# Last output tiles whole or in two column groups, warm-up products in banks of their own, and half of the last V copies ahead of q's transposition

## The chip, the cores and the metric

The kernel runs on one core of a Trainium2 chip. The time is that of the device, in microseconds, median of several executions; smaller is better. A core has five engines that run side by side and wait for each other through semaphores: TensorE (PE, matrix products; its loads of weights are shown as PEld), VectorE (DVE), ScalarE (ACT), GpSimd (POOL) and SyncE (SP, which here only issues DMAs). Products land in PSUM, which has 8 banks of 512 float32 values for each of 128 partitions; everything else lies in SBUF, and inputs and output in HBM.

## What is computed

Two blocks, one after the other. The first is an attention over 8 blocks of 96 positions, whose keys and values are mixed over blocks by a matrix P that five rounds of normalising rows and columns make (Sinkhorn). The second is a gated MLP whose gate is mixed over the positions:

```python
P = sort_net                                     # (4, 8, 8, 8)
for _ in range(5):
    P = exp(P - max(P, -1)); P /= sum(P, -1); P /= sum(P, -2)
k_s = einsum('bhij,bhjcd->bhicd', P, k_blocks)   # q, k, v: (4, 8, 768, 64)
v_s = einsum('bhij,bhjcd->bhicd', P, v_blocks)
x = softmax(q_blocks @ k_s.T / 8) @ v_s          # to (4, 768, 512)
u, v = split(relu(x @ w_in))                     # w_in (512, 1024)
v = (v - mean(v)) / sqrt(var(v) + 1e-6)
out = (u * (w_spatial @ v + b_spatial)) @ w_out  # (4, 768, 512), float32
```

## The kernel before

The work is cut into units, small functions named `u_XX`. The string ORDER (lines 16 to 48) lists them with their arguments, and the loop at the end of the kernel function calls them in that order; each engine gets its instructions in the order in which the units emit them, so ORDER is the schedule of every engine and queue at once. No planner changes it. A framework puts in semaphore waits where two instructions share a tile or a bank of PSUM. The first argument of most units is the first of the two PSUM banks they write (`ps_tile`, line 102), a letter says who copies the result out (A ScalarE, D VectorE, P GpSimd), then come the batch (0 to 3), and the head pair or chunk.

The four batches overlap: while batch 3 is in its attention, batch 2 is in its MLP. The units that matter here:

- `DM:bank:n:w` (L286) is n warm-up products of zeros ("dummies") of w columns. Nothing reads their result; they go to the first of the two banks.
- `SK` (L242) is one round of the normalisation on a tile of 32 x 64, on ScalarE (exp) and VectorE; the last one also transposes P. `PR`, `P0`, `PC`, `PD` spread P into the mixing matrices `pd`.
- `QT:bank:eng:b:hp:2` (L323) transposes q of one head pair by 12 products, over two banks. `KT` and `VT` (L338) mix and transpose k and v in one go. `LH:q:0:4:8` loads the second half of the first batch's q.
- `VM:bank:eng:b:hp` (L389) mixes v of a head pair, two products into two banks, and ScalarE or VectorE copies them to the tile `vm`. Each batch has four.
- `VC:b:ih` (L404) is four DMAs on SyncE's queue, which bring half of `vm` into the layout `vb` that the attention's second product reads; two VC make a batch. They need all four VM of the batch.
- `QX:eng:b` copies q to `qx` (L180, two instructions) and then issues a transposing DMA on SyncE's queue (L182) to `qX`. `XX:b:ih` is the transposing DMA of the attention's result (L189).
- `SC` (L422, exponential at L435) is the attention's first product, `AT` (L447) its second, which reads `vb`; `VP`, `UP` (L490, L535) are the products with w_in, `SP` (L547) and `SH` (L567) the mixing over positions with w_spatial, followed by the addition of the bias into `z` and the gate `gt` on VectorE or GpSimd. SP mixes a quarter of the channels over all positions, SH over half of the positions.
- The output of a batch is 6 chunks of 128 positions x 512 columns, each the sum of four products (mc 0 to 3) over `gt`. `OP` (L627) does two chunks at once. Only for the last batch `OF` (L588) does the first two products of a chunk ahead, while `gt` of mc 2 and 3 is not ready, and `OL` (L600) the other two, then a copy by ScalarE or VectorE and a store from SyncE's queue (L608). `OL:X` is the form for the very last chunk: ScalarE copies its left 256 columns and stores them from its own queue (L612, L614), VectorE the right 256, stored from SyncE's (L613, L615). `OH` (L617) is `OF` and `OL` of one chunk together; ORDER doesn't call it before.

On SyncE's queue near 85 to 105 us ORDER gives: XX:2:0, XX:2:1, QX:D:3, VC:3:1, VC:3:0. On PE in that place: SP:6:D:1:1, VM of head pair 2, SP:4:P:1:0, VM of pair 0, VM of pair 3, SP:0:P:1:2, two KT, VP, VM of pair 1, and two more VP. Of batch 3, the first AT reads half 1 of `vb`, the second half 0.

The last lines of ORDER hold the end: SP and SH of batch 3, then the chunks.

Of the kernel before, what the change touches and what calls it, by code (L numbers as in the profile page):

```python
# [8 lines left out]
FP32 = mybir.dt.float32  # L9
# [4 lines left out]


ORDER = """
IN LH:q:0:0:4 L:k:0:0:128 ID SK:0 MK SK:0 SK:0 QT:0:A:0:1:2 L:v:0:0:128 IV:1 SX DM:0:12:64
DM:1:12:64 DM:0:12:64 SK:0 SK:1 DM:1:12:64 QT:2:A:0:0:2 IV:0 LH:q:0:4:8 DM:0:12:64 PR:1 P0:0:2 L:wv
P0:4:6 P0:6:8 P0:2:4 L:wu L:v:1:0:128 PC:A L:k:1:0:128 L:ws DM:7:9:64 KT:2:D:0:0:2 KT:4:A:0:2:2
DM:7:2:64 KT:0:D:0:1:2 DM:7:1:64 VT:6:A:1:2 VT:2:D:0:2 SC:4:0:0:1 VT:0:D:2:2 PD:2:0:4 VX:7:D:1:1  # L20
QT:2:A:0:2:2 VX:4:A:0:1 VX:5:D:1:0 SC:0:0:1:1 VX:7:D:2:1 PD:1:0:4 PD:1:4:8 KT:2:D:0:3:2 PD:2:4:8
VX:4:D:0:0 PD:3:0:4 QT:6:A:0:3:2 VT:0:D:3:2 AT:2:P:0:0:1 L:q:1:0:128 SC:4:0:2:1 VX:7:D:2:0 SC:2:0:3:1
AT:0:D:0:1:1 SC:6:0:3:0 VX:4:D:3:1 VX:5:A:3:0 AT:2:D:0:2:1 SC:0:0:0:0 AT:6:D:0:3:1 XT:4:D:0:1:0
AT:2:P:0:3:0 SC:0:0:2:0 XT:7:D:0:1:1 L:v:2:0:128 AT:2:D:0:0:0 SC:4:0:1:0 AT:0:P:0:2:0 UP:6:A:0:0:1
AT:2:D:0:1:0 VP:0:A:0:5 VM:4:A:1:2 VM:6:D:1:1 XT:2:A:0:0:1 VM:0:D:1:0 XT:3:A:0:0:0 VP:4:A:0:3:4
VM:2:A:1:3 VP:0:A:0:2 VP:6:A:0:0:1 VC:1:0 LN:0:3:6 UP:2:A:0:1:1 L:k:2:0:128 WS:0:D:5 KT:6:A:1:1:2
KT:4:A:1:2:2 UP:2:A:0:0:0 LA:D:0:3 KT:6:D:1:0:2 PD:3:4:8 KT:4:A:1:3:2 QT:0:A:1:1:2 WS:2:D:4
QT:6:D:1:0:2 QT:4:A:1:2:2 QT:2:D:1:3:2 WS:0:D:3 LN:0:0:3 L:q:2:0:128 WS:1:D:0 SC:4:1:2:0 LA:P:0:5
LA:P:0:4 LA:P:0:1 SC:6:1:0:0 L:wo UP:2:D:0:1:0 VC:1:1 BB AT:0:P:1:2:0 AT:6:D:1:0:0 SC:4:1:1:0 SC:0:1:1:1
LA:P:0:2 VM:2:D:2:1 LA:P:0:0 VM:4:A:2:0 VM:6:D:2:2 SC:0:1:3:0 WS:2:D:2 SC:4:1:3:1 WS:3:D:1 VM:0:A:2:3  # L30
AT:6:D:1:1:0 AT:4:P:1:1:1 VC:2:0 SC:2:1:2:1 AT:0:D:1:3:1 AT:6:D:1:3:0 XX:1:0 SP:4:D:0:0 SC:0:1:0:1
AT:2:P:1:2:1 VC:2:1 QX:D:2 SP:6:D:0:2 AT:2:P:1:0:1 SP:4:D:0:1 SP:2:D:0:3 VP:6:A:1:0:1 KT:4:A:2:2:2
UP:0:A:1:1:0 KT:6:D:2:1:2 XX:1:1 KT:4:A:2:3:2 WT:x:1:1 L:v:3:0:128 KT:2:A:2:0:2 OP:0:D:0:0 SC:6:2:1:0
L:k:3:0:128 SC:2:2:2:0 VP:4:D:1:2:3 SC:2:2:2:1 SC:0:2:0:0 UP:6:A:1:1:1 AT:2:D:2:2:0 AT:4:P:2:1:0
LN:1:0:4 VP:0:A:1:4:5 UP:4:A:1:0:1 LA:D:1:2 SC:0:2:0:1 LA:P:1:3 SC:2:2:3:0 L:q:3:0:128 OP:6:A:0:2
LN:1:4:6 AT:0:D:2:0:0 AT:4:D:2:2:1 OP:2:D:0:1 LA:P:1:4 LA:D:1:5 LA:P:1:0 SC:0:2:1:1 SC:4:2:3:1
LA:D:1:1 UP:6:A:1:0:0 AT:0:D:2:0:1 AT:2:P:2:3:0 SP:4:D:1:3 AT:2:P:2:1:1 XX:2:0 AT:0:D:2:3:1
SP:6:D:1:1 VM:2:A:3:2 SP:4:P:1:0 VM:6:A:3:0 XX:2:1 VM:2:A:3:3 SP:0:P:1:2 QX:D:3 KT:2:A:3:3:2
KT:4:A:3:1:2 VP:6:A:2:0:1 VM:4:A:3:1 VP:2:A:2:4:5 VP:6:A:2:2:3 KT:2:A:3:0:2 KT:4:A:3:2:2 UP:0:A:2:0:1
LN:2:0:4 VC:3:1 UP:2:D:2:0:0 SC:4:3:3:0 LA:P:2:3 VC:3:0 SC:0:3:0:1 LA:D:2:2 UP:6:D:2:1:1 SC:4:3:3:1  # L40
SC:2:3:1:1 LA:D:2:1 UP:0:A:2:1:0 LA:P:2:0 AT:4:D:3:0:1 AT:6:D:3:3:0 LN:2:4:6 LA:P:2:4 OP:2:D:1:1
SC:4:3:1:0 SC:6:3:2:1 LA:D:2:5 OP:0:A:1:2 AT:6:D:3:2:1 AT:2:P:3:3:1 SP:4:D:2:0 AT:2:P:3:1:1
AT:6:P:3:1:0 SP:0:D:2:2 XX:3:1 SC:2:3:2:0 SC:4:3:0:0 OP:6:A:1:0 AT:0:D:3:0:0 AT:4:D:3:2:0 SP:2:P:2:1
SP:0:D:2:3 UP:2:A:3:1:1 VP:0:A:3:4:5 XX:3:0 UP:2:A:3:0:1 VP:4:A:3:2:3 LN:3:4:6 VP:2:A:3:0:1
OP:4:A:2:2 LA:P:3:4 LN:3:0:4 LA:P:3:3 LA:D:3:2 LA:D:3:0 LA:P:3:5 LA:P:3:1 UP:2:A:3:0:0 UP:0:A:3:1:0
OP:4:A:2:0 OP:0:A:2:1 SH:4:D:3:3:0 SP:2:D:3:0 SP:0:D:3:1 SP:2:D:3:2 SH:0:D:3:3:1 OF:1:3:1 OF:2:3:0
OF:3:3:2 OL:A:3:2 OL:D:3:0 OF:0:3:4 OL:D:3:4 OL:A:3:1 OF:2:3:3 OL:D:3:3 OF:0:3:5 OL:X:3:5
"""


# [9 lines left out]
def kernel(  # L60
# [12 lines left out]
    nc = tc.nc  # L73

    B, H, S, D = q.shape
# [5 lines left out]
    DM = H * D  # L81
# [3 lines left out]
    FC = DH // 128  # L85
# [9 lines left out]
    moe = ctx.enter_context(tc.tile_pool(name="moe", bufs=2))  # L95
# [3 lines left out]
    ps = psum.tile([128, 8, 512], FP32, name="ps")  # L99
    ps_bf = ps.rearrange("p x c -> p (x c)").bitcast(BF16).rearrange("p (x c) -> p x c", x=8)  # L100

    def ps_tile(n, dt=FP32):
        return (ps if dt == FP32 else ps_bf)[:, int(n):min(int(n) + 2, 8)]

    def copy(eng, out, in_):
        if eng == "A":
            nc.scalar.copy(out=out, in_=in_)  # L107
        else:
            nc.vector.tensor_copy(out=out, in_=in_)
# [26 lines left out]
    w_out_sb = const.tile([128, FC, DM], BF16, name="w_out_sb")  # L136
# [7 lines left out]
    st = {}  # L144
# [436 lines left out]
    def oh_mm(b, c, parts):  # L581
        for mc in parts:
            nc.tensor.matmul(  # L583
                st["oh", c][:, 0, :], lhsT=st["gt", b, mc][:, c * 128:(c + 1) * 128], rhs=w_out_sb[:, mc, :],
                start=(mc == EARLY[0]), stop=(mc == LATE[-1]),
            )
# [5 lines left out]
    def oh_tile():  # L592
        n = st["ohn"] = st.get("ohn", -1) + 1
        if n in (2, 3):
            return moe.tile([128, DM], FP32, name="oh_sb", tag="oh", bufs=2)
        if n % 2 == 0:
            st["oo"] = moe.tile([128, 2, DM], FP32, name="o_sb", tag="o", bufs=2)
        return st["oo"][:, n % 2]

    def u_OL(eng, b, c):  # L600
        b, c = int(b), int(c)
        oh_mm(b, c, LATE)
        t = st["oh", c][:, 0]
        o_sb = oh_tile()
        dst = out[b, c * 128:(c + 1) * 128, :]
        if eng in ("A", "D"):
            copy(eng, o_sb, t)
            nc.sync.dma_start(out=dst, in_=o_sb)  # L608
        else:
            h = DM // 2  # L610
            o2 = moe.tile([128, S], FP32, name="o2", tag="z", bufs=2)[:, 0:h]
            nc.scalar.copy(out=o_sb[:, 0:h], in_=t[:, 0:h])  # L612
            nc.vector.tensor_copy(out=o2, in_=t[:, h:DM])  # L613
            nc.scalar.dma_start(out=dst[:, 0:h], in_=o_sb[:, 0:h])  # L614
            nc.sync.dma_start(out=dst[:, h:DM], in_=o2)  # L615

    def u_OH(ps, eng, b, c):  # L617
        u_OF(ps, b, c)
        u_OL(eng, b, c)
# [55 lines left out]
```

## Time and profile before

| | |
|---|---|
| median of 3 runs | 157.74 us (157.69 to 157.99) |
| the profiled execution | 157.63 us |
| its span, first to last instruction | 155.9 us |
| PE busy | 140.2 us, 90% of the span |
| VectorE / ScalarE / GpSimd busy | 109.2 / 87.6 / 56.8 us |
| DMA | 25.50 MB, mean 164 GB/s; HBM read 24.78 MB, written 6.29 MB |
| granted PE clock over the span | 0.993 |

The difference of 1.7 us between the profiled execution and its span lies before the first and after the last instruction. "Busy" of PE counts a product as long as it is in the array; since products overlap, a busy PE is not one at its peak. Lines such as L447 are lines of the kernel; "SPq" or "ACTq" is the sequencer of an engine, which issues DMAs; `ps<-vb,ex` says what is written and read. In the timeline the columns are start and duration in us, engine, line, operation, tiles and the number of instructions; in brackets stands the idle time of the engine ahead, and what ended it.

### The profile page before, as it was taken

How to read it: one execution, taken by the hardware profiler on the slowest of the kernel's cores; microseconds unless marked ns; L12 is line 12 of the kernel's file. 1: busy time of each engine (PE TensorE's matmuls, PEld its weight loads, DVE VectorE, ACT ScalarE, POOL GpSimd, SP SyncE). 2: the span in 40 equal slices, each digit the busy share in tenths (PEclk: the TensorE clock that was granted, in tenths of full speed). 3: DMA queues.
4: the chain of work that ended last, by engine and by line, in shares of the span. 5: the costliest groups of instructions: out<-in, count | busy, mean ns of one | idle time of the engine just before them, and what ended most of it. 6: DMA issues, size and time to landing. Idle time of an engine off the chain costs nothing.

```text
span 155.9 us, 3816 instructions
## 1 busy us (share of the span) xinstructions
PE 140.2 (90%) x1553; PEld 87.6 (56%) x1564; DVE 109.2 (70%) x225; ACT 87.6 (56%) x132; POOL 56.8 (36%) x81
## 2 busy tenths in 40 slices
PE   0289999999989999999999999996999999999970
PEld 0188788646867665645556654663566554556520
DVE  3877889668789899648587958765568647328960
ACT  3224789888989430948864367983754247640030
POOL 7961944933146242022742271041051402610000
PEclk9999999999999999999999999999999999999997
DMA  2999999999999999979999934980438900342074
GB/s 14 194 203 207 204 205 204 210 207 206 247 275 206 205 229 229 201 131 143 204 196 267 264 55 81 173 158 3 155 114 132 209 0 0 135 165 109 0 263 145
DMA packets 36834, 25.50 MB, mean 164 GB/s; under 512 B 16592, under 2 KB 33744, under 8 KB 36816
## 3 DMA queue, kind: packets, MB, share of 16 engines
q0 software_dynamic: 14864, 12.19, 50.4%
q1 hardware_dynamic: 21808, 12.93, 34.3%
q8 instruction: 12, 0.20, 0.5%
q10 hardware_dynamic: 144, 0.13, 0.3%
q14 instruction: 6, 0.05, 0.1%
HBM read 24.78 MB, written 6.29 MB: 199 GB/s over the span
## 4 chain that ended last, share of the span: by engine, by line
PE 49%; DMA 25%; DVE 10%; POOL 4%; issue 4%; SPq 3%; ACT 1%; DVEq 0%; POOLq 0%; ACTq 0%
PE ps L547 13%; DMA v_in<-in_v_dram 12%; PE ps L627 9%; PE ps L490 8%; DMA q_in<-in_q_dram 8%; PE ps L535 6%; DVE z L553 4%; DVE gt L559 3%; PE ps L583 3%; PE ps L447 3%; DMA xT<-x_sb 3%; SPq L404 3%; DMA vb<-vm 2%; PE ps L422 2%; PE ps L389 1%
## 5 line engine op out<-in xcount | busy, mean ns | idle before, releaser
L547 PE MATMUL ps<-wspT,v_sb 128*128 128x384 bf16 x180 | 31.1, 326 | 0.0
L435 ACT ACTIVATE ex<-ps 96x768 bf16<-96x768 f32 x32 | 24.6, 806 | 9.2 <-PE ps L422 8.9
L459 POOL TENSOR_TENSOR x_sb<-xr,rec 96x512 bf16<-96x512 f32 x13 | 14.1, 1091 | 26.4 <-DVE rec L458 26.4
L535 PE MATMUL ps<-xT,w_in_sb 128*128 128x384 bf16 x128 | 23.2, 327 | 0.0
L547 PEld LDWEIGHTS <-v_sb 128*128 128x128 bf16 x180 | 17.0, 98 | 10.7
L490 PE MATMUL ps<-w_in_sb,xT 128*128 128x512 bf16 x91 | 22.1, 379 | 0.7 <-DMA xT<-x_sb 0.3
L504 DVE BATCH_NORM_STATS2 stats<-v_sb 128x6 f32<-128x512 bf16 x24 | 16.3, 677 | 8.4 <-ACT v_sb L113 8.3
L521 POOL TENSOR_SCALAR v_sb<-v_sb,nm,rstd 128x512 bf16<-128x512 bf16 x15 | 11.9, 792 | 20.1 <-ACT rstd L512 16.6
L553 DVE TENSOR_TENSOR z<-ps,b_bc 128x768 f32<-128x768 f32 x15 | 14.3, 956 | 6.2 <-PE ps L547 5.7
L113 ACT ACTIVATE v_sb<-ps 128x1024 bf16<-128x1024 f32 (+1 forms) x12 | 11.5, 954 | 9.9 <-PE ps L490 9.9
L627 PE MATMUL ps<-w_out_sb,gt 128*128 128x512 bf16 x67 | 16.6, 380 | 0.3
L535 PEld LDWEIGHTS <-w_in_sb 128*128 128x128 bf16 x128 | 11.8, 98 | 8.1
L490 PEld LDWEIGHTS <-xT 128*128 128x128 bf16 x96 | 8.9, 98 | 10.4 <-DMA xT<-x_sb 0.8
L113 ACT ACTIVATE u_sb<-ps 128x768 bf16<-128x768 f32 x13 | 10.5, 810 | 6.6 <-PE ps L535 6.1
L107 ACT COPY o_sb<-ps 128x1024 f32<-128x1024 f32 (+1 forms) x7 | 6.7, 952 | 12.3 <-DVE gt L576 8.8
L459 DVE TENSOR_TENSOR x_sb<-ps,rec 96x512 bf16<-96x512 f32 x19 | 13.0, 687 | 0.7
L447 PE MATMUL ps<-vb,ex 96*128 96x65 bf16 x256 | 11.7, 193 | 1.3 <-DMA vb<-vm 1.1
L447 PEld LDWEIGHTS <-ex 96*128 96x128 bf16 x256 | 10.2, 97 | 3.9 <-issue 1.2
L559 DVE TENSOR_TENSOR gt<-z,u_sb 128x768 bf16<-128x768 f32 x12 | 11.5, 958 | 0.4
L455 ACT COPY xr<-ps 96x520 f32<-96x520 f32 x13 | 7.6, 586 | 6.7 <-POOL x_sb L459 3.7
L323 PE MATMUL ps<-ident,q_in 128*64 128x128 bf16 x96 | 4.5, 244 | 6.9 <-DMA q_in<-in_q_dram 6.9
L627 PEld LDWEIGHTS <-gt 128*128 128x128 bf16 x72 | 6.6, 98 | 7.2
(91 smaller groups left out, 201.7 us busy)
## 6 DMA issues: line engine op xcount, KB each, us to landing
out_dram<-o_sb SPq DMA_DIRECT2D x9, 512.0 KB, 3.3
k_in<-in_k_dram POOLq DMA_DIRECT2D x4, 768.0 KB, 15.8
v_in<-in_v_dram POOLq DMA_DIRECT2D x4, 768.0 KB, 14.3
vb<-vm SPq DMA_DIRECT2D x24, 99.0 KB, 5.3
q_in<-in_q_dram POOLq DMA_DIRECT2D x3, 768.0 KB, 16.1
wsp_nat<-in_moe_w_spatial_dram POOLq DMA_DIRECT2D x1, 1152.0 KB, 25.7
w_in_sb<-in_moe_w_in_dram POOLq DMA_DIRECT2D x2, 512.0 KB, 13.9
q_in<-in_q_dram POOLq DMA_DIRECT2D x2, 384.0 KB, 8.5
```

Source lines behind the costliest of these rows:

```text
L113: nc.scalar.activation(out=out, in_=in_, func=AF.Relu)
L435: nc.scalar.activation(out=dst, in_=src, func=AF.Exp, scale=scale)
L447: nc.tensor.matmul(t[:, hh, ii * VW:ii * VW + D + 1], lhsT=e[:, c:c + 128], rhs=vb[b % 2][:, ih * NI + ii, 2 * hp + hh, 0:D + 1], start=Tr ...
L459: (nc.gpsimd if eng == "P" else nc.vector).tensor_mul(out=x_sb[:, hp].rearrange("p i (h d) -> p h i d", h=2), in0=tv[:, :, :, 0:D], in1=_r ...
L490: nc.tensor.matmul(t[:, x, :], lhsT=x_tile(b, n // 3)[:, kc, n % 3 * 128:(n % 3 + 1) * 128], rhs=w_in_sb[:, kc, DH:DFF], start=(kc == 0), ...
L504: nc.vector.bn_stats(out=stats, in_=v_sb[:, x, :])
L521: nc.gpsimd.tensor_scalar(out=v_sb, in0=v_sb, scalar1=nm[:, 0:1], scalar2=rs[:, n:n + 1], op0=ALU.add, op1=ALU.mult)
L535: nc.tensor.matmul(t[:, x, 0:HW], lhsT=w_in_sb[:, kc, mc * 128:(mc + 1) * 128], rhs=x_tile(b, ih)[:, kc], start=(kc == 0), stop=(kc == KC ...
L547: nc.tensor.matmul(t[:, x, 0:HW], lhsT=st["v_sb", b, n][:, mc * 128:(mc + 1) * 128], rhs=wspT[:, n, x * HW:(x + 1) * HW], start=(n == 0), ...
L553: nc.vector.tensor_add(out=z.rearrange("p (x c) -> p x c", x=2), in0=t[:, :, 0:HW], in1=b_bc.rearrange("p (x c) -> p x c", x=2),)
L559: eng.tensor_mul(out=gt, in0=z, in1=st["u", b, mc // 2][:, mc % 2])
L627: nc.tensor.matmul(t[:, x, :], lhsT=st["gt", b, mc][:, c * 128:(c + 1) * 128], rhs=w_out_sb[:, mc, :], start=(mc == 0), stop=(mc == FC - 1),)
```

## The change

Three parts, all by ORDER, the third with a new unit.

1. The dummies. There were 72: five groups of 12 in banks 0 and 1, which QT:0 and PR use too, and 9, 2 and 1 in bank 7 around the first KT. There are 60 now, in five groups in banks 4 and 5. The second QT comes ahead of all of them, and SK rounds stand otherwise in between.
2. VC:3:1 is issued ahead of QX:D:3. For that the VM of head pair 1 of batch 3 comes ahead of SP:0:P:1:2, in banks 6 and 7, where it was in banks 4 and 5 behind the first VP of batch 2.
3. The last chunks. Chunks 2, 0 and 1 are begun in OF and ended in OL as before, but in that order without others in between; chunks 4 and 3 are done whole (OH) in banks of their own, 4 and 5; chunk 5, the last, is done by the new unit OX in two groups of four products of 256 columns, the left in bank 6, the right in bank 7, each with its own copy and store. `OL` loses its form X.

```diff
 ORDER (pieces that differ)
-... IV:1 SX DM:0:12:64 DM:1:12:64 DM:0:12:64 SK:0 SK:1 DM:1:12:64 QT:2:A:0:0:2 IV:0
-    LH:q:0:4:8 DM:0:12:64 PR:1 P0:0:2 ...
+... IV:1 SX SK:0 QT:2:A:0:0:2 DM:4:12:64 DM:5:12:64 DM:4:12:64 DM:5:12:64 DM:4:12:64 SK:1 IV:0
+    LH:q:0:4:8 PR:1 P0:0:2 ...
-... L:ws DM:7:9:64 KT:2:D:0:0:2 KT:4:A:0:2:2 DM:7:2:64 KT:0:D:0:1:2 DM:7:1:64 VT:6:A:1:2 ...
+... L:ws KT:2:D:0:0:2 KT:4:A:0:2:2 KT:0:D:0:1:2 VT:6:A:1:2 ...
-... VM:6:A:3:0 XX:2:1 VM:2:A:3:3 SP:0:P:1:2 QX:D:3 KT:2:A:3:3:2 KT:4:A:3:1:2
-    VP:6:A:2:0:1 VM:4:A:3:1 VP:2:A:2:4:5 ... UP:0:A:2:0:1 LN:2:0:4 VC:3:1 UP:2:D:2:0:0 ...
+... VM:6:A:3:0 XX:2:1 VM:2:A:3:3 VM:6:A:3:1 SP:0:P:1:2 VC:3:1 QX:D:3 KT:2:A:3:3:2 KT:4:A:3:1:2
+    VP:6:A:2:0:1 VP:2:A:2:4:5 ... UP:0:A:2:0:1 LN:2:0:4 UP:2:D:2:0:0 ...
-... OF:3:3:2 OL:A:3:2 OL:D:3:0 OF:0:3:4 OL:D:3:4 OL:A:3:1 OF:2:3:3 OL:D:3:3 OF:0:3:5 OL:X:3:5
+... OF:3:3:2 OL:A:3:2 OL:D:3:0 OL:A:3:1 OH:4:D:3:4 OH:5:A:3:3 OX:6:3:5

 def u_OL(eng, b, c):
...
-        if eng in ("A", "D"):
-            copy(eng, o_sb, t)
-            nc.sync.dma_start(out=dst, in_=o_sb)
-        else:
-            h = DM // 2
-            o2 = moe.tile([128, S], FP32, name="o2", tag="z", bufs=2)[:, 0:h]
-            nc.scalar.copy(out=o_sb[:, 0:h], in_=t[:, 0:h])
-            nc.vector.tensor_copy(out=o2, in_=t[:, h:DM])
-            nc.scalar.dma_start(out=dst[:, 0:h], in_=o_sb[:, 0:h])
-            nc.sync.dma_start(out=dst[:, h:DM], in_=o2)
+        copy(eng, o_sb, t)
+        nc.sync.dma_start(out=dst, in_=o_sb)
+
+    def u_OX(ps, b, c):
+        b, c = int(b), int(c)
+        t = ps_tile(ps)
+        h = DM // 2
+        dst = out[b, c * 128:(c + 1) * 128, :]
+        for x in range(2):
+            for mc in range(FC):
+                nc.tensor.matmul(
+                    t[:, x, 0:h], lhsT=st["gt", b, mc][:, c * 128:(c + 1) * 128],
+                    rhs=w_out_sb[:, mc, x * h:(x + 1) * h], start=(mc == 0), stop=(mc == FC - 1),
+                )
+            o_sb = moe.tile([128, S], FP32, name="o2", tag="z", bufs=2)[:, 0:h]
+            copy("AD"[x], o_sb, t[:, x, 0:h])
+            (nc.scalar, nc.sync)[x].dma_start(out=dst[:, x * h:(x + 1) * h], in_=o_sb)
```

## The prediction

> **What bounds the kernel now.** I read the page's slices first, then the chain of waits, then the timeline round each place that the change touches, last the stretches by windows. The slices:
>
> ```profile
> PE   0289999999989999999999999996999999999970
> DMA  2999999999999999979999934980438900342074
> ```
>
> From about 12 us to 148 us TensorE (PE) is full but for one slice of 6 (the 28th, 105 to 109 us); the DMA engines are full from 4 to about 86 us but for one slice, and busy again near the end. So a microsecond is worth something where PE stands still, or where PE itself waits for a full DMA. The chain of waits names both:
>
> ```profile
> 5.63 11.81 DMA q_in<-in_q_dram
> ...
> 27.30 19.41 DMA v_in<-in_v_dram
> ...
> 102.95 3.45 DMA vb<-vm
> ...
> 145.80 5.14 PE ps L583 x23
> ...
> 151.01 0.38 ACT o_sb L612
> 151.39 0.02 issue
> 151.41 0.42 DVE o L613
> ```
>
> Two loads set the first 47 us: the second half of the first q lands at 17.44, v of batch 2 at 46.72. A gap in PE for the copies of the last V ends at 106.40. The end is the last product (L583), two copies one after the other (L612, L613), then a store.
>
> The timeline in the middle:
>
> ```profile
> 88.50 0.81 PE L389 MATMUL ps<-v_in,pd 128*128 128x384 bf16 x4
> 89.02 1.50 ACT L107 CAST vm<-ps 128x768 bf16<-128x768 f32 x2 [1.47 <-PE ps L389]
> 89.15 2.11 PE L547 MATMUL ps<-wspT,v_sb 128*128 128x384 bf16 x12
> ...
> 92.17 2.47 DVE L180 COPY qx<-q_in 128x1536 bf16<-128x1536 bf16 x2
> ...
> 94.72 3.70 SPq L182 DMA_TRANSPOSE qX<-qx  x1
> ...
> 98.46 5.08 SPq L404 DMA_DIRECT2D vb<-vm  x8
> ...
> 104.79 0.53 PE L447 MATMUL ps<-vb,ex 96*128 96x65 bf16 x11
> ...
> 106.44 0.31 PE L447 MATMUL ps<-vb,ex 96*128 96x65 bf16 x5 [1.13 <-DMA vb<-vm]
> ```
>
> SyncE's queue issues q's transposition (3.70 us) and then eight V copies (5.08); the last copy is issued at 102.95 and lands at 106.40, while PE has stood at the twelfth of sixteen L447 products. These start about 32 ns apart, (0.53 - 0.19)/10, so the next would have started at 105.15: PE loses 1.29 us.
>
> The end, in stretches (columns: engines' busy time, then clock, DMA share, GB/s):
>
> ```profile
> 148.40:149.20 0.80, 0.80 (x5) 0.38 (x4) 0.63 (x2) 0.03 (x1) 0.00 (x0) 1.00 0.04 10
> 149.20:150.20 1.00, 1.00 (x6) 0.48 (x5) 0.40 (x2) 0.59 (x1) 0.00 (x0) 1.00 0.91 336
> 150.20:151.20 1.00, 0.72 (x4) 0.11 (x2) 0.59 (x1) 0.19 (x1) 0.00 (x0) 1.00 1.04 389
> 152.20:153.20 1.00, 0.00 (x0) 0.00 (x0) 0.00 (x0) 0.00 (x0) 0.00 (x0) 1.00 1.01 359
> ```
>
> The reader is to see that from 0.8 us after the first store is issued (148.46) to about 153.4 the DMA engines are full, although PE ends at 150.9: the six stores of 256 KB queue.
>
> And the start:
>
> ```profile
> 8.27 2.72 PE L289 MATMUL ps<-warm 128*128 128x64 bf16 x48 [0.89 <-ACT qT L107]
> 10.91 0.85 PE L323 MATMUL ps<-ident,q_in 128*64 128x128 bf16 x12
> 11.70 0.82 PE L289 MATMUL ps<-warm 128*128 128x64 bf16 x12
> 17.48 0.53 PE L323 MATMUL ps<-ident,q_in 128*64 128x128 bf16 x12 [0.33 <-DMA q_in<-in_q_dram]
> ```
>
> Twelve equal L323 products took 0.85 us at 10.91 and 0.53 at 17.48: PE is slow at first.
>
> **What the Trainium skill says.** "TensorE: Matmul & The Clock Gate", Part 1, says that the array runs at half clock until it has been busy for a whole activity window of about 3.4 us, and that the window runs free; the L323 pair (0.85 against 0.53) agrees that there is a ramp, the window's length no view here shows. "PSUM — Partial Sum Buffer", the section on bank collisions, has any two engines that share a bank guarded by a semaphore; the trace agrees at the end, where VectorE's half copy (L613) starts at 151.41, 0.02 after ScalarE's half of the same bank. "DMA: Bandwidth & Descriptors", section "Issuing engines are not separate DMA queues", says that DMAs of all issuers run on the same 16 engines; the share of 1.01 to 1.04 with stores from two queues agrees.
>
> **The change part by part.** All sums are made against the profiled execution, 157.63 us with a span of 155.9; its 157.63 stands 0.11 under the median 157.74, to which I carry the difference.
>
> 1. Dummies. PE had 60 dummies up to 12.5 us and 12 more up to 15.1 (L289); it gets 60 in banks 4 and 5. The first no longer waits 0.89 us for the copy of QT, whose banks 0 and 1 it used. PE's new order: two QT groups from 6.52 (about 0.64 each, twelve at 53 ns), then 60 x 0.053 = 3.2, so it is idle from about 11.0. PR waits for VectorE's SK chain, whose transposed P is ready at 11.87 in the timeline; PR started at 12.45 behind a DM group and now can at 11.9, half a microsecond sooner. ScalarE copies the second qT (0.80) between two exponentials; it has 1.51 idle there, so that costs nothing. But PE reaches the second half of q, which lands at 17.44 whatever PE does: it waited 0.49 there and would wait about a microsecond. Other engines may save a little of the lead; that dies at 46.72, where v lands behind a full DMA. Gain 0. On the other side PE reaches that place with 0.46 us to spare (its last start before, 46.26, plus one issue, against 46.76), so a delay costs only beyond that. Bounds: 0 to +1.1 (rival A); I take 0.
>
> 2. VM of head pair 1 moved up, in front of SP:0:P:1:2, into banks 6 and 7. VM:6:A:3:0 just before uses the same banks; ScalarE's copy of it runs 89.02 to 89.77 (half of the 1.50). So the moved VM can't start at 89.15, where L547 starts now, but at about 89.82: a stall of 0.67, new. Behind it on PE stand twelve L547, two KT, two VP and so everything. Its own two products (0.33) are moved, not added: they leave 93.72. So L547 starts 1.0 later, all behind the old place 0.67 later. ScalarE's copy of the moved VM runs about 90.5 to 91.3, before the KT copies (91.76, 1.23 idle before them): hidden. Cost +0.67; bounds +0.55 to +0.8.
>
> 3. V copies. VC for half 1 can be issued from about 91.3: four at 5.08/8 = 0.64 are done at 93.9. q's transposition waits for VectorE's qx copies, which end 92.17 + 2.47 = 94.64 and come 1.0 later with the z before them: SyncE issues it at 95.7, so the four ahead of it delay nothing. It ends at 99.4, and the four others follow, the last issued at 101.3, landing 2.8 to 3.5 later (the answer for vb in this stretch gives 2.7/2.8/3.5): 104.1 to 104.8. PE needs it at 105.15 + 0.67 = 105.82. The stall of 1.29 goes. What is late next: qX. It landed 5.5 us after issue, now 101.2; its first reader, the SC group seen at 101.09, is due at 101.76. Slack 0.56; if it takes the other transposition's 6.3, PE loses 0.2.
> Sum of 2 and 3: +0.67 - 1.29 = -0.62. From 106.4 to 138 PE is busy 31.34 of 31.60, with no load in the chain, so this travels to the end. Bounds: -0.75 to -0.2.
>
> 4. The end. PE's work is equal: chunk 5 in eight products of 256 columns in place of four of 512. The skill's clock-gate page, "Back-to-back issue gap", gives N/2.4 + 2.5 ns, so 0.109 against 0.216 each as an estimate; the trace's L583 rows are 5.14/23 = 0.22. The last product stays at about 150.9. What changes is behind it: the first half is done 0.43 earlier, ScalarE copies it while PE makes the second, and VectorE's half needn't wait for ScalarE: the last store is issued at about 151.42 in place of 151.86, 0.44 sooner. But stores: the first issue (148.46) and the bytes are unchanged, six chunks of 256 KB = 1.57 MB at about 375 GB/s are 4.2 us, 149.3 to 153.4, and the engines have no pause in it before or after (the new issues, about 149.3, 150.0, 150.7, 151.1 and 151.4, all come ahead of the drain). So the 0.44 is spent in the queue. Bounds 0.1 lost to 0.44 gained; I take 0.05 gained.
>
> Sum: 0 + 0.67 - 1.29 - 0.05 = -0.67: span 155.2, profiled 156.96, median 157.74 - 0.67 = 157.1.
>
> **Rivals.**
> A. Slower: the clock. The old dummies kept PE dense from 8.3 to past 13.4; the new leave it idle from about 11.0 to 11.9, and nearly so to 12.7. If the window falls so that PE is still slow, the 72 L338 of 13.4 to 17 cost 53 in place of 30 ns, +1.65, small ones +0.3, less 0.66 for the earlier KT and 0.49 of q's wait: 0.8 late at 17.5; slow for two more microseconds adds about 1.1; the stalls at 46 us (0.46 and 0.33) give back 0.8. +1.1, with -0.67 about 158.2. It decides only if PE is over 0.8 late near 46 us. For it: the 0.85/0.53 pair. Against: QT and dummies are now one dense stretch of 4.5 us, and VectorE, not PE, is full from 14 to 18.
> B. The middle is eaten: qX or the last V lands late (+0.2 to 0.4), or the bank wait is longer. About 157.55. For it: the slack of 0.56. Against: DMA share of only 0.39 in 90 to 98 us.
> C. The end pays in full: stores flow as soon as they are issued, -0.44 in place of -0.05: 156.7. Against: the share of 1.0.
> That the change doesn't do what it says: the moved copies are in front of the transposition on SyncE, and DM uses no bank of QT; I hold that excluded.
>
> **How the numbers follow.** Forecast 0.58 (157.1, own range 156.85 to 157.35), C 0.15 (156.7), B 0.17 (157.55), A 0.10 (158.2). The 0.2% that a measurement of this kernel can tell is 0.32 us. Faster by more: forecast nearly whole and C, 0.73. Within: B and little of A, 0.18. Slower: 0.09, from A. The range leaves out A and half of what lies beyond C: 156.5 to 157.75.
>
> **What would show it.** Right: no idle before L447 behind vb; a new idle of about 0.6 in PE at about 89.2 released by ScalarE's vm; vb issues in two groups of four about the transposition; DMA share near 1.0 from 149 to 153, shifted by 0.6, the last landing about 2.5 us or more after an earlier issue; a longer wait for q_in near 17. Wrong: L323 or L338 products at 53 ns after 14 us and no wait at 46.7 (A), a wait on qX (B), or a last store landing about 1.0 sooner than 154.6 (C).

## The result and the profile after

| | before | after |
|---|---|---|
| median of the comparison (6 executions each) | 157.91 us (157.69 to 158.63) | 156.55 us (156.37 to 156.62) |
| ratio, 95% interval | | 0.9904 [0.9886, 0.9923] |
| the profiled execution | 157.63 us | 156.58 us |
| its span | 155.9 us | 154.8 us |

The gain is about 1.4 us by the medians and 1.05 between the two profiled executions; the forecast was 0.67. (The profiled execution of before, 157.63, was quicker than all six of the comparison. The account below by traces covers the 1.05; what makes up the other 0.3 isn't shown.) The slices of the page of the kernel after:

```profile
PE   0377999999998999999999989999999999999970
PEclk9997799999999999999999999999999999999998
DMA  2999999999999999949999985950428800342074
```

The 6 that PE had in the 28th slice is gone. New is the pair of 7 in the clock row near 12 to 19 us: here the records have PE at half clock from 13.75 to 17.16 us.

The middle, in the timeline of the kernel after:

```profile
88.07 0.81 PE L389 MATMUL ps<-v_in,pd 128*128 128x384 bf16 x4
88.59 2.21 ACT L107 CAST vm<-ps 128x768 bf16<-128x768 f32 x3 [1.48 <-PE ps L389]
89.45 0.48 PE L389 MATMUL ps<-v_in,pd 128*128 128x384 bf16 x2 [0.57 <-ACT vm L107]
89.77 1.62 PE L547 MATMUL ps<-wspT,v_sb 128*128 128x384 bf16 x9
...
105.08 0.65 PE L447 MATMUL ps<-vb,ex 96*128 96x65 bf16 x16
```

and on SyncE's queue alone:

```profile
90.82 2.61 SPq L404 DMA_DIRECT2D vb<-vm  x4
95.32 3.65 SPq L182 DMA_TRANSPOSE qX<-qx  x1
99.02 2.52 SPq L404 DMA_DIRECT2D vb<-vm  x4
```

All as forecast: the moved VM waits for ScalarE's copy (0.57 of idle time behind the end of the product before; 0.73 by the starts, against a product that follows at once), the V copies go in two groups about the transposition, and the sixteen L447 products run through. By PE's starts this stretch is 0.59 us shorter than before, against a forecast of 0.62.

The end, in stretches with the columns used before:

```profile
148.20:149.20 1.00, 1.00 (x8) 0.59 (x6) 0.69 (x1) 0.09 (x1) 0.00 (x0) 1.00 0.94 348
149.20:150.20 1.00, 0.71 (x7) 0.39 (x4) 0.26 (x1) 0.77 (x2) 0.00 (x0) 1.00 1.03 377
150.20:151.20 1.00, 0.00 (x0) 0.00 (x0) 0.17 (x1) 0.00 (x0) 0.00 (x0) 1.00 1.04 385
151.20:152.20 1.00, 0.00 (x0) 0.00 (x0) 0.00 (x0) 0.00 (x0) 0.00 (x0) 1.00 1.01 354
```

Again the DMA engines are full from the moment that the stores flow. From the first store's issue to the last landing it takes 6.07 us (147.43 to 153.50) against 6.11 before (148.46 to 154.57): 0.04 gained, 0.05 forecast.

That makes 0.63 of the 1.07 by which the last landing is earlier. The rest lies where no part of the change is. Before, PE stood for 0.50 us at 68.65 at a transposition of the attention's result (xT of batch 1); after, it doesn't:

```profile
68.64 0.55 PEld L490 LDWEIGHTS <-xT 128*128 128x128 bf16 x4 [0.83 <-DMA xT<-x_sb]
68.65 1.04 PE L490 MATMUL ps<-w_in_sb,xT 128*128 128x512 bf16 x4 [0.34 <-DMA xT<-x_sb]
```

```profile
67.79 1.46 PE L490 MATMUL ps<-w_in_sb,xT 128*128 128x512 bf16 x6
68.01 0.75 PEld L490 LDWEIGHTS <-xT 128*128 128x128 bf16 x4
```

(The first fence is the timeline of the kernel before, the second of the kernel after.) The transposition was issued at the same moment, 63.61 and 63.63, but landed at 68.60 before and 67.54 after. The view of DMA traffic from 65 to 69 us, in 40 slices of 0.1 us, shows how. Its row counts the time of a packet, the piece in which a DMA engine moves data, in the slice where the packet begins. Before:

```profile
DMA  9999999999999990000010000099994000000000
...
q8 instruction: 1, 0.02, 1.5%
```

After:

```profile
DMA  9999999999999999999910000000000000000000
...
q8 instruction: 1, 0.02, 1.6%
```

Before, next to no packet begins from 66.5 to 67.6, and the rest follows in a burst; after, the transfer runs through to 67.1. In both there is one packet of queue 8, kind "instruction", 16,384 bytes. Its record has it at 65.89 to 66.85 before, in the midst of the transposition, and at 66.98 to 68.02 after, when only 24 of the transposition's packets had still to end; they did so by 67.09. From this comes theory F: the fetch of a block of instructions holds up the DMA that it meets, and part 1 moved the fetches.

That they are fetches for PE is worked out from the page: 12 such packets are 196,608 bytes, and PE and PEld have 2 x 1556 = 3112 instructions in the kernel after, so one block is about 259 of them; no other engine has more than 224. The Trainium skill, "Runtime: NRT & Kernel Launch", section "Instruction fetch mechanics", says that a sequencer fetches blocks of 16 KiB (256 instructions) over a DMA queue of its own and that the cost of crossing into a new one is "mostly hidden". The size agrees; the experiments below show a cost that isn't hidden. Twelve dummies fewer are 24 instructions fewer (product and weight load). Between the fetches at 55.9 and 67.0 us one instruction takes 11.1/256 = 0.043 us, so by this estimate the block boundary there comes 24 x 0.043 = 1.0 us later; the fetch near 66 came 1.1 later. The same holds near 104 us: before, a fetch at 104.22 to 105.13 fell into the last V copy, which took 3.45 us where the one ahead took 2.77. So part of the gap of 1.29 that the forecast put down to the order of the V copies may have been the fetch's as well. Not every fetch moved: those near 40.8 and 47.5 us stayed within 0.1 us; the second lies just behind PE's wait for v at 46.8.

### The profile page after: what moved, and what is told of

Its sections match the earlier page's. It is cut to its first block, busy times and chain, and to the rows that moved or that the text cites. A ratio compares the mean times of both kernels' runs of the same rounds, so it can differ in the third digit from the quotient of the medians.

```text
span 154.8 us, 3814 instructions
## 1 busy us (share of the span) xinstructions
PE 140.4 (91%) x1556; PEld 87.9 (57%) x1556; DVE 108.7 (70%) x224; ACT 88.0 (57%) x133; POOL 56.7 (37%) x81
## 4 chain that ended last, share of the span: by engine, by line
PE 70%; DMA 14%; DVE 7%; issue 3%; POOL 2%; ACT 1%; DVEq 0%; POOLq 0%
PE ps L547 19%; DMA v_in<-in_v_dram 13%; PE ps L535 10%; PE ps L635 10%; PE ps L490 10%; PE ps L338 5%; PE ps L447 4%; PE ps L422 4%; PE ps L583 3%; POOL x_sb L459 1%; PE ps L389 1%; PE ps L567 1%; DMA p_all<-in_sort_net_dram 1%; DVE p_all L246 1%; DVE colsum L247 1%
## 5 line engine op out<-in xcount | busy, mean ns | idle before, releaser
L547 PE MATMUL ps<-wspT,v_sb 128*128 128x384 bf16 x180 | 31.1, 326 | 0.0
L547 PEld LDWEIGHTS <-v_sb 128*128 128x128 bf16 x180 | 17.0, 98 | 10.7
L490 PE MATMUL ps<-w_in_sb,xT 128*128 128x512 bf16 x96 | 22.2, 379 | 0.0
L521 POOL TENSOR_SCALAR v_sb<-v_sb,nm,rstd 128x512 bf16<-128x512 bf16 x15 | 11.8, 788 | 20.1 <-ACT rstd L512 16.6
L107 ACT COPY o_sb<-ps 128x1024 f32<-128x1024 f32 (+1 forms) x8 | 7.2, 905 | 13.5 <-DVE gt L576 8.9
L490 PEld LDWEIGHTS <-xT 128*128 128x128 bf16 x96 | 8.9, 97 | 10.0 <-DMA xT<-x_sb 0.2
L447 PEld LDWEIGHTS <-ex 96*128 96x128 bf16 x256 | 10.1, 97 | 2.7 <-DVE x_sb L459 0.2
L447 PE MATMUL ps<-vb,ex 96*128 96x65 bf16 x256 | 11.5, 193 | 0.1
L422 PEld LDWEIGHTS <-kT 64*96 64x96 bf16 x256 | 7.7, 122 | 4.8 <-issue 4.0
```

The lines of the kernel that those rows point to most:

```text
L422: nc.tensor.matmul(t[0:BLK, hh, ii * 128:ii * 128 + BLK], lhsT=kT[rows, i * BLK:(i + 1) * BLK], rhs=rhs, start=True, stop=True,)
L447: nc.tensor.matmul(t[:, hh, ii * VW:ii * VW + D + 1], lhsT=e[:, c:c + 128], rhs=vb[b % 2][:, ih * NI + ii, 2 * hp + hh, 0:D + 1], start=Tr ...
L490: nc.tensor.matmul(t[:, x, :], lhsT=x_tile(b, n // 3)[:, kc, n % 3 * 128:(n % 3 + 1) * 128], rhs=w_in_sb[:, kc, DH:DFF], start=(kc == 0), ...
L521: nc.gpsimd.tensor_scalar(out=v_sb, in0=v_sb, scalar1=nm[:, 0:1], scalar2=rs[:, n:n + 1], op0=ALU.add, op1=ALU.mult)
L547: nc.tensor.matmul(t[:, x, 0:HW], lhsT=st["v_sb", b, n][:, mc * 128:(mc + 1) * 128], rhs=wspT[:, n, x * HW:(x + 1) * HW], start=(n == 0), ...
```

## The experiments

The theories: R, the sum on record, in which the dummies (step 1) are worth nothing and the bank wait and the V copies (steps 2 and 3) together 0.62; and F. Rivals of F were chance, that the landing varies whatever the program (C in the first four expectations), that the early dummies cost by themselves (S), and the clock (C in the two later expectations that name it). Each ratio is to the kernel before in the same comparison; its median was 157.98 us beside p1, p2, p3 and c60, 158.38 beside p13, a72_more, a48 and a_banks, and 158.33 beside p12, after_again and a72_mid. In some kernels ORDER takes two lines fewer, so that their line numbers are smaller by 2 (L445 for L447).

### One part of the change at a time

**p1_dummies**: the kernel before with the change's first part alone.

```diff
-IV:1 SX DM:0:12:64 DM:1:12:64 DM:0:12:64 SK:0 SK:1 DM:1:12:64 QT:2:A:0:0:2 IV:0 LH:q:0:4:8 DM:0:12:64 PR:1
+IV:1 SX SK:0 QT:2:A:0:0:2 DM:4:12:64 DM:5:12:64 DM:4:12:64 DM:5:12:64 DM:4:12:64 SK:1 IV:0 LH:q:0:4:8 PR:1
-L:ws DM:7:9:64 KT:2:D:0:0:2 KT:4:A:0:2:2 DM:7:2:64 KT:0:D:0:1:2 DM:7:1:64
+L:ws KT:2:D:0:0:2 KT:4:A:0:2:2 KT:0:D:0:1:2
```

> The kernel before with part 1 of the change alone (60 dummies in banks 4 and 5, nothing around the first KT). Theory R (as on record): the start is covered by the load of q and of v, so 0, within 0.2 us. Theory F (fetch): PE has 24 instructions fewer, so each fetch of its next instructions over the DMA engines comes about 1 us later; the one at 65.9 us then no longer falls into the transposition of batch 1's result, which lands about 1 us sooner, and PE's wait of 0.5 us at 68.6 goes; -0.45 us, and up to 0.6 more if the fetch at 104.2 leaves the last V copy too. Theory C (chance): that landing varies from run to run whatever the program; 0 in the median, and the wait seen in some runs of both.

Measured: 156.60 us (156.37 to 157.51), ratio 0.9914 [0.989, 0.9937]. The part that was priced at nothing brings by itself about as much as the whole change. Its trace has the fetch at 67.20, xT landed at 67.52 and no wait there; and the last V copy took 2.79 us, with the fetch of that place beginning only at 105.17, so the gap behind it is half of what it was, though all eight copies still stand behind q's transposition:

```profile
104.52 0.54 PE L445 MATMUL ps<-vb,ex 96*128 96x65 bf16 x11
...
105.52 0.31 PE L445 MATMUL ps<-vb,ex 96*128 96x65 bf16 x5 [0.46 <-DMA vb<-vm]
```

(0.46 of idle time; 0.63 by the products' starts, where it was 1.29.)

**c60**: the kernel before without the 12 dummies in bank 7 round the first KT, all else as it was.

```diff
-L:ws DM:7:9:64 KT:2:D:0:0:2 KT:4:A:0:2:2 DM:7:2:64 KT:0:D:0:1:2 DM:7:1:64
+L:ws KT:2:D:0:0:2 KT:4:A:0:2:2 KT:0:D:0:1:2
```

> The kernel before with only the 12 dummies of bank 7 around the first KT left out; the other 60 stay where they were, in banks 0 and 1. F: the same as part 1 alone, -0.45 us or more, since only the number of PE's instructions matters; no wait at 68.6, the fetch there near 67. R and a theory that the banks or the order of the dummies matter: 0 or slower. C: 0.

Measured: 156.53 us (156.44 to 157.50), ratio 0.9914 [0.989, 0.9937]: the same as p1_dummies. So of part 1 neither the banks nor the places make a difference that can be measured, only that twelve are left out. Two of the six executions took 157.35 and 157.50, and the traced one is the second of these. In it the loads land about a microsecond late, v at 47.78 where it was 46.72 before; why isn't known. It has no wait behind xT (fetch at 67.55, landing at 68.42) and 0.57 at vb, and from v's landing to the end of the span it takes 107.95 us, where the kernel before took 109.14.

**p2_vcopies**: the kernel before with the second part alone.

```diff
-VM:2:A:3:3 SP:0:P:1:2 QX:D:3 ... VP:6:A:2:0:1 VM:4:A:3:1 ... LN:2:0:4 VC:3:1
+VM:2:A:3:3 VM:6:A:3:1 SP:0:P:1:2 VC:3:1 QX:D:3 ... VP:6:A:2:0:1 ... LN:2:0:4
```

> The kernel before with part 2 alone (VM of pair 1 moved up, four V copies ahead of q's transposition). R: -0.6 us: a new wait of PE of 0.7 us behind ScalarE's copy of VM near 89 us, and none before L447 at 106. F: the same, with the wait at 68.6 still there (72 dummies). C: the same in the median, the wait at 68.6 there or not. If the copies' place were worth nothing: 0.

Measured: 157.20 us (157.10 to 157.37), ratio 0.994 [0.9926, 0.9954]: 0.78 below the 157.98 of before in that comparison, where the forecast for this part was 0.62. The new wait is 0.73, the gap at vb is gone. The wait behind xT is still there, 0.70, with the fetch at 65.96 and xT landed at 68.81.

**p3_tail**: the kernel before with the third part alone.

```diff
-OL:D:3:0 OF:0:3:4 OL:D:3:4 OL:A:3:1 OF:2:3:3 OL:D:3:3 OF:0:3:5 OL:X:3:5
+OL:D:3:0 OL:A:3:1 OH:4:D:3:4 OH:5:A:3:3 OX:6:3:5
```

> The kernel before with part 3 alone (the last chunks). R: -0.05 us, within 0.2: the last store is issued 0.4 us sooner but lands as late, because the stores' DMA engines are full from the first store on; 4.2 us from the first packet to 153.4. Rival (stores flow): -0.44 us. F and C say nothing else of it.

Measured: 158.37 us (158.10 to 158.60), ratio 1.0022 [1.001, 1.0033]. A miss for R and for its rival: slower by 0.35. But in the traces the tail isn't where it is lost. The first store is issued at 149.09, already 0.63 later than in the trace of before, and from there to the last landing it takes 6.12 us, as before (6.11). Nearly all of the 0.63 comes from two longer waits ahead:

```profile
68.89 1.04 PE L490 MATMUL ps<-w_in_sb,xT 128*128 128x512 bf16 x4 [0.56 <-DMA xT<-x_sb]
...
107.10 0.31 PE L447 MATMUL ps<-vb,ex 96*128 96x65 bf16 x5 [1.50 <-DMA vb<-vm]
```

By the starts they are 0.73 behind xT (0.50 before) and 1.66 at vb (1.29). The two fetches fell 0.5 and 0.7 us later than in the profiled execution of before, at 66.41 and 104.92, still within the transfers, and the last V copy took 3.84. Why the same instructions are fetched later here stays open, and so does the 0.35 between the medians: the one trace of before is an execution 0.35 quicker than its median in this comparison.

The parts don't add: 1.38 for the first and 0.78 for the second make 2.16, and the whole is 1.4.

### Putting the parts together

**p13_no_v**: parts 1 and 3 without part 2, to see what the V copies are worth once the fetch lies elsewhere (the diff of p1_dummies and that of p3_tail together).

> The kernel before with parts 1 and 3 of the change, without part 2 and the V copies. Theory R (the sum on record: part 1 is worth 0, the V copies with their bank wait 0.62): without them 0.6 is lost against the kernel after, about 157.2. Theory F (PE's instruction fetch lies elsewhere once early dummies are gone, so the last V copy is quick by itself and the gap behind it only about 0.6, as large as the bank wait that part 2 brings): the same as the kernel after and as part 1 alone less 0.04, 156.5 to 156.6; a fetch at about 67 us, no wait behind the transposition at 68, a gap of 0.5 to 0.7 behind vb and no wait of 0.7 at 89.

Measured: 156.62 us (156.54 to 156.64), ratio 0.9889 [0.9874, 0.9904]. F to the tenth; R said 157.2. The gap at vb is 0.72 and there is no wait at 89. So part 2 takes away a gap of 0.6 to 0.7 and puts in one of 0.73: beside part 1 it is worth nothing that can be measured (ratio 0.9889 without it, 0.9904 with it, and the intervals overlap).

**p12_old_tail**: the kernel after with the tail of before (the diffs of p1_dummies and p2_vcopies), beside the kernel after itself on the same chip, **after_again**.

> The kernel after with the tail of the kernel before (parts 1 and 2 without part 3). Theory R (stores drain at the DMA engines' rate whatever is issued sooner): 0.05 slower than the kernel after, 156.5 to 156.7, which can't be told from it. Theory T (the tail pays in full): 0.44 slower, 156.9 to 157.0; then the last landing stands 6.5 us behind the first store's issue in place of 6.1.

> The kernel after, unchanged, beside the other two of this call on the same chip. All theories: 156.4 to 156.7.

Measured: 156.47 us (156.37 to 156.72), ratio 0.9887 [0.9865, 0.9909], and 156.65 us (156.33 to 157.59), 0.9904 [0.9875, 0.9933]. The tail pays nothing. Without it the end of the chain has the two copies one after the other, as before:

```profile
149.97 0.38 ACT o_sb L610
150.35 0.02 issue
150.37 0.42 DVE o L611
```

and the last store is issued at 150.82 in place of 150.40; it lands at 153.49, against 153.50 in the kernel after. The 0.42 are spent in the queue.

### Moving the fetch back

**a72_more_dummies**: the kernel after with twelve more dummies at the start, in the change's own bank.

```diff
-DM:4:12:64 DM:5:12:64 DM:4:12:64 DM:5:12:64 DM:4:12:64 SK:1
+DM:4:12:64 DM:5:12:64 DM:4:12:64 DM:5:12:64 DM:4:12:64 DM:5:12:64 SK:1
```

> The kernel after with one more group of 12 dummies at the start, in its own bank, so that PE has 72 again as before. Theory F: PE's instruction fetch comes about 0.55 us earlier for 12 products and their 12 weight loads, at about 66.4, inside the transposition that is issued at 63.6; its landing moves from 67.5 towards 68.6 and the wait of 0.5 to 0.7 at about 68.6 comes back: 156.9 to 157.2. The middle stays as in the kernel after. Theory R (dummies are covered by the loads of q and v): no change, 156.5, fetch or no fetch. Theory C (the clock: more dummies keep PE fast at 13.8 to 17.2): PE waits for q and v anyway, no change either, 156.5.

Measured: 157.14 us (157.08 to 157.90), ratio 0.993 [0.9912, 0.9948]. The wait is back:

```profile
68.83 1.04 PE L490 MATMUL ps<-w_in_sb,xT 128*128 128x512 bf16 x4 [0.41 <-DMA xT<-x_sb]
```

with the fetch at 66.45 and xT landed at 68.78. The clock record, which begins at 10.32 us here, has no half-clock stretch, and the kernel was still 0.6 us slower than after.

**a72_mid**: the same twelve, but far from the start, where PE waits for v anyway.

```diff
-LA:P:0:2 VM:2:D:2:1
+LA:P:0:2 DM:2:12:64 VM:2:D:2:1
```

> The kernel after with 12 dummies more, not at the start but ahead of the VM that waits for the load of v at 46.8 (0.3 us of dummies in a wait of 0.5 to 0.9). Theory F (only the place of the fetch in PE's instruction stream counts): all instructions behind stand 24 further on, the fetch comes at about 66.4 again, the transposition issued at about 63.6 lands at 68.6 to 68.9 and the wait of 0.5 to 0.7 behind it returns: 157.0 to 157.2. Theory S (it is the dummies of the first 16 us that cost, through the clock or the order of the lead): no change, 156.5, with the transposition landing at 67.5.

Measured: 157.21 us (157.05 to 157.29), ratio 0.9931 [0.9912, 0.9951], the same. The lead is that of the kernel after to the instruction, so S falls: what counts is the number of instructions ahead of the place, not where they stand. (after_again, in the same comparison, had four of six executions at 156.33 to 156.66, all six here are at 157.05 to 157.29; because of its two long ones, below, the intervals of the ratios overlap, and the wait in the traces carries the reading.) Its DMA traffic from 65 to 69 us:

```profile
DMA  9999999999999999998000000000000595000000
...
q8 instruction: 1, 0.02, 1.4%
```

Again more than a microsecond in which no packet begins, then a burst, and PE waits:

```profile
69.01 0.61 PE L490 MATMUL ps<-w_in_sb,xT 128*128 128x512 bf16 x2 [0.53 <-DMA xT<-x_sb]
```

**a48_fewer_dummies**: the kernel after with one group of twelve fewer.

```diff
-DM:4:12:64 DM:5:12:64 DM:4:12:64 DM:5:12:64 DM:4:12:64 SK:1
+DM:4:12:64 DM:5:12:64 DM:4:12:64 DM:5:12:64 SK:1
```

> The kernel after with one group of 12 dummies fewer, 48. Theory F: the fetch comes at about 67.6, behind the transposition's landing at 67.5; nothing more to gain there, and the last V copies lie before the fetch near 106: 156.5, no wait at 68. Theory R: 156.5 as well. Theory C (the clock): PE is idle longer before 12 us, so the half clock lasts longer; if PE is then late at the load of v near 46.8, up to 1 us slower, 156.8 to 157.5, with products at 53 ns behind 17 us.

Measured: 156.77 us (156.37 to 157.23), ratio 0.9903 [0.9884, 0.9921], not to be told from the kernel after; the half clock lay at 12.77 to 16.18, and PE still waited 0.71 for v at 46.90. It doesn't tell F from R. The slow products behind 17 us that C allowed aren't in its trace.

All traces together, by the fetch's start after the issue of that transposition (us; the table is taken from the records of the traces):

| kernel | fetch behind issue | landing behind issue |
|---|---|---|
| p2_vcopies | 2.19 | 5.04 |
| before | 2.28 | 4.99 |
| a72_mid | 2.76 | 5.29 |
| p3_tail | 2.88 | 5.31 |
| a72_more_dummies | 2.93 | 5.26 |
| c60 | 3.20 | 4.07 |
| p12_old_tail | 3.28 | 3.86 |
| a48_fewer_dummies | 3.30 | 3.93 |
| after | 3.35 | 3.91 |
| a_banks (below) | 3.41 | 3.91 |
| after_again | 3.41 | 5.44 |
| p13_no_v | 3.52 | 4.01 |
| p1_dummies | 3.54 | 3.86 |

There is a step between 2.93 and 3.20: with a fetch that comes in time to meet it the transposition takes 1.1 to 1.4 us longer than its usual 3.9. All five kernels with 72 dummies lie on the slow side and seven of the eight with fewer on the other, which speaks against chance. The one exception lies at the edge. after_again is the kernel after, and two of its six executions, the profiled one among them, took 157.47 and 157.59, the other four 156.33 to 156.66. In the profiled one the fetch ran from 67.02 to 68.02; all packets of the transposition but two had ended by 67.08, and the last ended at 68.04, behind the fetch. Two of some 2,500 were enough for a landing at 69.05 and a wait of 1.04 at L490:

```profile
69.10 0.61 PE L490 MATMUL ps<-w_in_sb,xT 128*128 128x512 bf16 x2 [0.87 <-DMA xT<-x_sb]
```

So the change has moved the fetch only just past the transposition, and here it was met all the same. The other long execution isn't traced, and c60's trace shows that about 157.5 can also come from late loads.

At another transposition of the same traces, the one issued near 116 us, the move works the other way. In the five kernels with 72 dummies a fetch begins 0.3 to 0.6 us behind its issue, and it lands after 4.1 to 4.3 us; in the eight with fewer the fetch begins 3.4 to 3.9 behind it, and it takes 5.4 to 5.9. In the kernel after PE came to its first product with this data at 121.19, 0.26 after the landing, so the loss stays hidden; in a48_fewer_dummies, where it lands at 121.46, the chain of waits goes through it. For the V copy at 103 us the records say the same: where the fetch begins 1.3 and 1.7 us behind the issue of the last copy (before, p3_tail) it takes 3.45 and 3.84, where it begins 2.3 to 2.5 behind (c60, p13_no_v, p1_dummies) 2.77 to 2.88.

### A version without the new wait

**a_banks**: the kernel after, with the moved VM put a little further ahead, into banks 4 and 5, and its neighbours' banks changed to fit. The work is the same.

```diff
-VM:2:A:3:2 SP:4:P:1:0 VM:6:A:3:0 XX:2:1 VM:2:A:3:3 VM:6:A:3:1 SP:0:P:1:2 VC:3:1
+VM:2:A:3:2 VM:4:A:3:1 SP:0:P:1:0 VM:6:A:3:0 XX:2:1 VM:2:A:3:3 SP:4:P:1:2 VC:3:1
-KT:4:A:3:1:2
+KT:0:A:3:1:2
```

> The kernel after with the moved VM (head pair 1 of batch 3) one unit pair earlier, in banks 4 and 5, and SP:4:P:1:0 and SP:0:P:1:2 with their banks exchanged accordingly, so that no VM follows another in banks 6 and 7. The same work. If the wait of 0.73 at 89.45 is due to the bank and travels to the end: 155.8, ratio to before about 0.987, no wait above 0.2 near 89. If what comes behind it takes the place of the wait (the exchange of banks makes KT or VP wait for GpSimd's z, or q's transposition is late at the first SC): 156.2 to 156.6.

Measured: 155.57 us (155.44 to 155.75), ratio 0.9824 [0.9808, 0.984]. It beats both kernels, the one after by about 1.0 us by the medians of different comparisons; the intervals of the ratios don't overlap. In its timeline L547 follows the VM at once, and the V copies start no later:

```profile
88.57 0.81 PE L389 MATMUL ps<-v_in,pd 128*128 128x384 bf16 x4
...
89.10 1.50 ACT L107 CAST vm<-ps 128x768 bf16<-128x768 f32 x2 [1.12 <-PE ps L389]
89.22 2.11 PE L547 MATMUL ps<-wspT,v_sb 128*128 128x384 bf16 x12
...
90.63 1.28 SPq L404 DMA_DIRECT2D vb<-vm  x2
```

So the wait of 0.73 was the bank's, and it travelled to the end: the first store is issued at 146.59, where it was 147.43. The remaining 0.2 to 0.3 of the gain by the medians isn't accounted for.

## Why the prediction was right or wrong

The direction was right, the size not: 0.67 forecast, 1.05 in the profiles, 1.36 by the medians of the comparison.

**Step 1, "Gain 0", is what failed.** It asked what the dummies cover and what the clock makes of their absence, and found a load that hides all of it. That much held: p1_dummies and the kernel after pass the load of v at 46.8 no sooner than the kernel before. (Its sentence that q "lands at 17.44 whatever PE does" did not: q landed at 16.04. In the traces of before and p2_vcopies, with a fetch at 15.35 and 15.37, it landed at 17.44 and 17.47; in p3_tail, with the fetch at 15.48, at 15.97, in all those with the fetch at 16.4 to 16.6 at 15.9 to 16.1, and in c60, where all loads were late, at 17.08. This looks like the same thing at another place, free because v comes later; no run tests it.) But the term left out is that PE has 24 instructions fewer, so that later fetches come at other places: near 66 and 104 us, 1.1 and 1.2 later. By itself this brought 1.4 us (p1_dummies, c60), where the step's bounds allowed no gain at all (0 to 1.1 slower). The traces show the wait behind xT, 0.50, and some 0.6 of the gap at vb. The 0.50 was in the profile of before, in the timeline and in the row of L490; since no part of the change stood there, I didn't ask why its transfer was late.

**Steps 2 and 3** came out: 0.73 for the bank wait (0.67 forecast, bounds 0.55 to 0.8), the gap of 1.29 gone, together 0.59 in the profile (0.62), and 0.78 alone on the kernel before. q's transposition was issued at 95.32 (95.7) and landed 5.5 us later, so rival B's late qX didn't come. What the step couldn't see is that about half of the 1.29 was the fetch's: beside part 1 the two moves cancel (p13_no_v).

**Step 4** was right: stores that are issued sooner wait in full queues (0.04 in the profile, nothing in p12_old_tail). Rival C is out.

**Rival A** had the right mechanism and the wrong price. In the profiled execution PE did fall back to half clock, from 13.75 to 17.16 us; the traces of p1_dummies and after_again show such a stretch too, those of p12_old_tail and a_banks, with the same start, don't. The price can be read from p12_old_tail: there PE came to q's second half at 16.60, in the kernel after at 17.53, so the fall cost 0.9 us at this place, where rival A had 0.8. (The forecast's own sign, a longer wait for q near 17 us, wasn't seen: q landed at 16.04, and PE didn't wait.) But at 46.83 both still waited for v, 0.49 us in the kernel after and 0.65 in p12_old_tail, so nothing of it reached the end: 156.58 and 156.54 us for the two traced executions. The sum on record for A, 1.1 us, counted a further delay behind 17 us that didn't come.

## What to carry to other kernels

When instructions are added to PE or taken away from it, even idle ones, look up the "instruction" packets in the trace and what they meet: later ones move, and a transfer that PE waits for may be met or freed tens of microseconds further on, while another one comes to be met in its place. Price an edit alone and together with the others before it gets the credit, since two edits can shorten the same gap. A producer that is moved ahead needs a bank that is free at its new place; giving it one was worth another 1.0 us here.

## What wasn't expected of the hardware

- In these 13 traces an instruction fetch of 16,384 bytes took 0.9 to 1.7 us, and the transposition near 64 us landed 1.1 to 1.5 us later, of 3.9, when the fetch met it. Two packets left behind the fetch sufficed.
- In before, p2_vcopies, p3_tail and a72_mid no packet of the transposition ends from 0.4 to 0.5 us behind the fetch's start until the fetch is over. Then 27 or 28 packets end one by one, about 0.03 us apart, and when they are done some 20 others, begun 1.2 to 1.5 us earlier, end together and the burst follows. It looks as if one DMA engine stood still for the fetch and the others then waited for it to catch up. The Trainium skill, "DMA: Bandwidth & Descriptors", section "Queues, rings and completion order", says that a DMA engine takes turns between its queues and drains a whole packet before it switches; that would make the packets queued behind the fetch wait for it, but no view here shows which engine carried which packet. Why the others should wait isn't shown.
- The fetch's place varies with the execution: in the five kernels with 72 dummies it began 2.19 to 2.93 us behind the transposition's issue. In after_again, where it began within 0.1 us of the transfer's end, the traced execution took 157.47 us and four others 156.33 to 156.66.
- PE's granted clock fell to half for one stretch of 3.41 us in four traces (13.75 to 17.16 in the kernel after), although PE was busy for 7 tenths or more of every slice of that page from 7.7 us on. Other executions with the same start show no such stretch.
